# Attention over a cached K and V: probabilities transposed in 32x32 blocks by VectorE, the first 16 units' values by pairs, and a quarter of wo projected earlier

**Chip and metric.** One core of one Trainium2 chip. The time is that of the device for one launch, in microseconds (us). Executions carry a state, fast or slow (a slow one lies over 1.5% above the fastest of its kernel); only fast ones are compared, and each ratio is to the kernel before as it ran in the same job. PE is TensorE, DVE is VectorE, ACT is ScalarE, SP issues the loads.

## The reference, cut

```python
B, Sq, D = 8, 4, 512
Hq, Hkv, Sk, Dh = 32, 8, 2048, 128
q = (x @ wq).reshape(B, Sq, Hq, Dh).transpose(0, 2, 1, 3)
k, v = (jnp.repeat(t, Hq // Hkv, axis=1) for t in (k_cache, v_cache))
p = softmax(einsum("bhqd,bhkd->bhqk", q, k) * Dh ** -0.5)
o = einsum("bhqk,bhkd->bhqd", p, v)
return o.transpose(0, 2, 1, 3).reshape(B, Sq, Hq * Dh) @ wo      # all bfloat16
```

K and V are 33.5 MB each, wq and wo 4.2 MB each: 75.5 MB are read for little arithmetic.

## The kernel before

The work is cut into 32 units: one pair of K/V heads of one batch, 1 MB of K and 1 MB of V. For each unit PE transposes K (as f32 words, two bf16 in one), DVE copies the result out of PSUM (`kt`), PE makes scores, ACT takes the exponential and its row sums, PE transposes the probabilities back so that keys lie on the partitions, ACT copies those to `probs`, and PE multiplies with V. `norms` turns the row sums into reciprocals, once for two units.

```python
def transpose_part(u, t):                 # four parts to a unit
    for j in range(JT):
        nc.tensor.transpose(kp[:, j, :], k4[:, w : w + 128], ident4[:, :])
    nc.vector.tensor_copy(out=k_t..., in_=kp...)               # 128x1024 bf16
...
def probs_to_keys(u):
    for j in range(JT):
        nc.tensor.transpose(pt[:, j, :], s_sbs[u][:, j, :, :]..., ident[:, :])
    for g in range(2):
        nc.scalar.copy(out=pr[rows, :, g, :], in_=pt[rows, :, :]...)
...
def values(u):                            # 32 matmuls of 32 columns
    for i in range(C):
        nc.tensor.matmul(o_ps[:, :], lhsT=vs[u][:, 2 * (t * JT + j) + c, :], rhs=pr[:, i, :, :]..., ...)
...
for n in range(NU + A):                   # A = 2: values run two units behind the K transposes
    w = n - A
    transpose_part(n, 0..1); scores(n - 1); transpose_part(n, 2..3)
    if w >= 0:
        values(w)
        if w % 2 == 0: norms(w)
        finish(w)
    probs_to_keys(n - 1)
    load_ready(...)                       # lets SP issue what may be issued
```

A `manual_schedule` keeps the order of the source.

The softmax here doesn't subtract the row's maximum and nothing guards it: scores larger than these inputs give would overflow.

## Time and profile before

| | before |
|---|---|
| time, median of three runs | 190.3 us (189.22 to 192.44) |
| span of the profiled run | 187.5 us |
| PE, DVE, ACT busy | 78%, 59%, 37% |
| bytes of the load queue | 75.55 MB, 96.3% of the span of 16 DMA engines |

### The profile page before, as it was taken

Reading aid. Unit: us, or ns where it says so; the run is one execution under the profiler, and the core shown is the slowest. Engines: PE = TensorE matmul, PEld = TensorE weight load, DVE = VectorE, ACT = ScalarE, POOL = GpSimd, SP = SyncE. Lnnn points to the kernel's source line nnn. Section 1 sums busy time; section 2 is a strip of 40 time slices with the busy share of each in tenths; the row PEclk is TensorE's granted clock in tenths of the full one; section 3 lists DMA queues with packets and bytes.
Section 4 is the critical chain, followed back from the end, with each engine's and each line's share of the span. In section 5 each row is a group of like instructions: output and inputs, shape, how many; then the busy total and the mean of one; then the engine's idle time right before and its main releaser. Section 6 shows DMA issues by size and latency. Waiting matters only on the chain.

```text
span 187.5 us, 5467 instructions
## 1 busy us (share of the span) xinstructions
PE 146.1 (78%) x2386; PEld 118.4 (63%) x2386; DVE 110.0 (59%) x225; ACT 69.1 (37%) x200; POOL 4.6 (2%) x9
## 2 busy tenths in 40 slices
PE   0524789999999788898788888788799888887382
PEld 0511248888797667786676766666587677666271
DVE  0850376878877566587565657575277766674020
ACT  2001146446464443153444443423344443435200
POOL 8100000000000000000000000000000000000000
PEclk9999999999999999999999999999699999999879
DMA  5998999999999999999999999999999999999970
GB/s 203 468 447 376 426 425 426 426 419 425 426 423 425 419 428 425 426 423 426 428 419 426 425 426 421 432 421 423 423 426 421 428 425 421 426 425 404 400 292 14
DMA packets 10983, 75.90 MB, mean 405 GB/s; under 512 B 1288, under 2 KB 1448, under 8 KB 2600
## 3 DMA queue, kind: packets, MB, share of 16 engines
q1 hardware_dynamic: 10912, 75.55, 96.3%
q8 instruction: 18, 0.29, 0.6%
q14 instruction: 5, 0.04, 0.1%
q10 hardware_dynamic: 48, 0.02, 0.0%
HBM read 75.53 MB, written 0.03 MB: 403 GB/s over the span
## 4 chain that ended last, share of the span: by engine, by line
DMA 81%; PE 13%; DVE 2%; issue 1%; ACT 1%; SPq 0%
DMA k_sb<-in_k_cache_dram 50%; DMA v_sb<-in_v_cache_dram 10%; DMA wo_m<-in_wo_dram 9%; DMA x_sb<-in_x_dram 7%; PE kp L199 6%; DMA wo_sb<-in_wo_dram 4%; PE psq L220 2%; PE s_ps L269 2%; DVE kt L201 1%; PE qtp L230 1%; ACT q_nat L227 1%; PE pse L244 1%; PE pt L288 0%; PE l_ps L311 0%; PE o_ps L329 0%
## 5 line engine op out<-in xcount | busy, mean ns | idle before, releaser
L201 DVE COPY kt<-kp 128x1024 bf16<-128x1024 bf16 x128 | 82.6, 685 | 35.2 <-PE kp L199 35.1
L199 PE MATMUL kp<-ident,k_sb 128*128 128x128 f32 x512 | 73.2, 289 | 20.0 <-DMA k_sb<-in_k_cache_dram 18.4
L199 PEld LDWEIGHTS kp<-ident,k_sb 128*128 128x128 f32 x512 | 58.6, 147 | 31.7 <-issue 15.9
L294 ACT COPY probs<-pt 64x512 bf16<-64x512 bf16 x64 | 37.1, 579 | 52.7 <-PE pt L288 52.3
L280 ACT ACTIVATE s_sb<-s_ps 128x256 bf16<-128x256 f32 x64 | 23.9, 379 | 30.6 <-PE s_ps L269 19.9
L329 PE MATMUL o_ps<-probs,v_sb 128*128 128x32 bf16 x1024 | 30.7, 177 | 1.7 <-DMA v_sb<-in_v_cache_dram 1.7
L329 PEld LDWEIGHTS <-v_sb 128*128 128x128 bf16 x1024 | 29.9, 96 | 3.0 <-DMA v_sb<-in_v_cache_dram 2.2
L269 PE MATMUL s_ps<-kt,q_bd 128*32 128x256 bf16 x512 | 21.3, 286 | 0.0
L269 PEld LDWEIGHTS <-q_bd 128*32 128x32 bf16 x512 | 10.8, 96 | 6.4 <-issue 5.5
L319 DVE RECIPROCAL r_sb<-l_ps 128x64 f32<-128x64 f32 x16 | 8.9, 557 | 8.6 <-PE l_ps L311 8.6
L280 ACT ACTIVATION_READ_ACCUMULATOR s_sb<-s_ps 128x1 f32 x64 | 12.7, 198 | 0.0
L288 PE MATMUL pt<-ident,s_sb 128*128 128x128 bf16 x128 | 12.3, 218 | 0.0
L311 PE MATMUL l_ps<-by_gq,ones 128*128 128x64 f32 x32 | 6.9, 297 | 5.3 <-DVE by_gq L304 5.3
L340 DVE TENSOR_TENSOR oT<-o_ps,r_sb 128x32 bf16<-128x32 f32 x32 | 6.1, 191 | 6.3 <-PE o_ps L329 5.7
L311 PEld LDWEIGHTS l_ps<-by_gq,ones 128*128 128x128 f32 x32 | 4.8, 188 | 6.8 <-DVE by_gq L304 5.0
L288 PEld LDWEIGHTS <-s_sb 128*128 128x128 bf16 x128 | 8.9, 104 | 0.0
L227 ACT ACTIVATE q_nat<-psq 128x512 bf16<-128x512 f32 x2 | 1.2, 597 | 18.7 <-PE psq L220 18.7
L304 DVE TENSOR_TENSOR by_gq<-l_sb,by_q 128x64 f32<-128x64 f32 x16 | 3.4, 216 | 2.1 <-ACT s_sb L280 2.1
L236 DVE COPY qT_all<-qtp 128x128 bf16<-128x128 bf16 x8 | 1.2, 216 | 5.8 <-PE qtp L230 5.8
L220 PE MATMUL psq<-wq_sb,xT_sb 128*32 128x512 bf16 x32 | 3.8, 628 | 0.3 <-DVE xT_sb L214 0.3
L461 ACT CAST out_sb<-out_ps 64x256 bf16<-64x256 f32 x1 | 0.4, 365 | 9.8 <-PE out_ps L405 9.8
L211 PE MATMUL xtp<-ident,x_sb 32*128 32x32 bf16 x4 | 0.3, 191 | 4.4 <-DMA x_sb<-in_x_dram 4.4
(48 smaller groups left out, 45.2 us busy)
## 6 DMA issues: line engine op xcount, KB each, us to landing
k_sb<-in_k_cache_dram SPq DMA_DIRECT2D x32, 1024.0 KB, 19.6
v_sb<-in_v_cache_dram SPq DMA_DIRECT2D x32, 1024.0 KB, 12.7
wq_sb<-in_wq_dram SPq DMA_DIRECT2D x1, 4096.0 KB
wo_sb<-in_wo_dram SPq DMA_DIRECT2D x4, 512.0 KB
wo_sb<-in_wo_dram SPq DMA_DIRECT2D x4, 256.0 KB, 8.2
wo_m<-in_wo_dram SPq DMA_DIRECT2D x1, 640.0 KB
wo_e<-in_wo_dram SPq DMA_DIRECT2D x8, 40.0 KB
wo_n<-in_wo_dram SPq DMA_DIRECT2D x1, 64.0 KB, 18.4
```

What stands on the lines that cost most here:

```text
L199: nc.tensor.transpose(kp[:, j, :], k4[:, w : w + 128], ident4[:, :])
L201: nc.vector.tensor_copy(out=k_t[:, :, :, :].rearrange("k j s e -> k (j s e)"), in_=kp[:, :, :].rearrange("k j s -> k (j s)").bitcast(BF16),)
L220: nc.tensor.matmul(psq[k * T : (k + 1) * T, :], lhsT=xT_sb[:, r, :], rhs=wq_sb[:, r, n : n + rep * Dh], start=(r == 0), stop=(r == R - 1),)
L269: nc.tensor.matmul(s_ps[t * 32 : (t + 1) * 32, :, g, :], lhsT=q_bd[:, p, e, b, g, :, :], rhs=kt[(u, t)][:, :, g * 64 : (g + 1) * 64, e], s ...
L280: nc.scalar.activation(out=s_sb[:, :, g, :], in_=s_ps[:, :, g, :], func=EXP, accum_out=l_sbs[u][:, u % 2, g : g + 1])
L288: nc.tensor.transpose(pt[:, j, :], s_sbs[u][:, j, :, :].rearrange("q g s -> q (g s)"), ident[:, :])
L294: nc.scalar.copy(out=pr[rows, :, g, :], in_=pt[rows, :, :].rearrange("s j (c q) -> s (j c) q", q=HQ),)
L304: nc.vector.tensor_tensor(out=by_gq[:, :, :, :], in0=l_sbs[u][:, :, :].unsqueeze(3).to_broadcast([128, 2, 2, HQ]), in1=by_q[:, :].unsqueez ...
L311: nc.tensor.matmul(l_ps[:, :, :].rearrange("d u q -> d (u q)"), lhsT=ones[:, :], rhs=by_gq[:, :, :, :].rearrange("k u g q -> k (u g q)"), ...
L319: nc.vector.reciprocal(r_sb[:, :, :], l_ps[:, :, :])
L329: nc.tensor.matmul(o_ps[:, :], lhsT=vs[u][:, 2 * (t * JT + j) + c, :], rhs=pr[:, i, :, :].rearrange("s g q -> s (g q)"), start=(i == 0), s ...
L340: nc.vector.tensor_tensor(out=oT[(p + 1) // 2][:, :, (p == 2) * 1, b, :], in0=o_pss[u][:, :].rearrange("d (h s) -> d h s", h=HP), in1=r_sb ...
```

## The change

It takes work from PE and ACT, and is meant to shorten what follows the last loads. Not shown in the cut: the scores are laid out for transposes within 32x32 blocks, one exponential of 512 columns replaces two of 256, the PSUM space of the old transposes goes to a fourth buffer for `kp`, and the loads of the first quarter of wo are put into the list of the other loads, at the place in which they already stood. Its core:

```diff
-    for j in range(JT):
-        nc.tensor.transpose(pt[:, j, :], ...)
     for g in range(2):
-        nc.scalar.copy(out=pr[rows, :, g, :], in_=pt[rows, :, :]...)
+        nc.vector.transpose(out=pr[rows, :, g, :], in_=s_sbs[u][rows, :, :]...)   # 32x32 blocks
...
-    nc.vector.tensor_copy(out=k_t..., in_=kp...)
+    (nc.scalar.copy if part == 3 else nc.vector.tensor_copy)(out=kt[(u, t)]..., in_=kp...)
...
+def values2(u):                            # units u and u + 1 together, first 16 units
+    for i in range(2):
+        nc.vector.tensor_tensor(out=by_row[:, i, :, :, :], in0=l_sbs[u]..., in1=by_q..., op=mult)
+    nc.tensor.matmul(l_ps[:, :], lhsT=by_row..., rhs=ones[:, 0:1], ...)
+    nc.vector.reciprocal(r_sb[:, :], l_ps[:, :])
+    for c in range(0, C, 2):
+        for i in range(2):                 # 256 columns each
+            nc.tensor.matmul(o_ps[i * 64 : (i + 1) * 64, :], lhsT=probs[(u + i) % 3][:, c : c + 2, :, :]...,
+                             rhs=vs[u + i][:, c : c + 2, :]..., ...)
+    nc.scalar.mul(out=o_sb..., in_=o_ps[:, :], mul=r_sb[:, 0:1])
+def finish2(u): ...                        # two f32 matmuls fold the halves into oT
...
     transpose_part(n, 2..3)
+    probs_to_keys(n - 1)                   # was the last thing of the step
     if w >= 0:
-        values(w) ...
+        if w >= NU - NS: values(w) ...     # NS = 16
+        elif w % 2 == 1: values2(w - 1)
-    probs_to_keys(n - 1)
-    load_ready(min(n + 1, NU), max(w + 1, 0))
+    load_ready(min(n + 1, NU), max(w + 1 if w >= NU - NS else (w + 1) // 2 * 2, 0))
...
     if w == NU - 2:
         project(0, WE, WM + 1)
+        project(1, 0, 8)
-to_tokens(2); project(1, 0, 4); to_wo_rows(2); project(1, 4, 4)
+to_tokens(2); to_wo_rows(2)
```

More of the change, by code (lines that the diff above doesn't have):

```diff
@@ L38 @@
     J = C // 2
-    JT = J // 4
+    JT = J // 2
+    NS = 16
     HP = 2 * rep
@@ L60 @@
     vpool = ctx.enter_context(tc.tile_pool(name="vpool", bufs=VB))
-    ktpool = ctx.enter_context(tc.tile_pool(name="ktpool", bufs=6))
+    ktpool = ctx.enter_context(tc.tile_pool(name="ktpool", bufs=3))
     small = ctx.enter_context(tc.tile_pool(name="small", bufs=2))
-    psum_k = ctx.enter_context(tc.tile_pool(name="psum_k", bufs=3, space=bass.MemoryType.PSUM))
+    psum_k = ctx.enter_context(tc.tile_pool(name="psum_k", bufs=4, space=bass.MemoryType.PSUM))
     psum_s = ctx.enter_context(tc.tile_pool(name="psum_s", bufs=1, space=bass.MemoryType.PSUM))
-    psum_t = ctx.enter_context(tc.tile_pool(name="psum_t", bufs=1, space=bass.MemoryType.PSUM))
     psum_o = ctx.enter_context(tc.tile_pool(name="psum_o", bufs=1, space=bass.MemoryType.PSUM))
@@ L99 @@
     ident = const.tile([128, 128], BF16, name="ident")
-    by_q = const.tile([128, HQ], FP32, name="by_q")
+    by_q = const.tile([128, 2, HQ], FP32, name="by_q")
+    fold = const.tile([128, 2, 2, NQ], FP32, name="fold")
     ones = const.tile([128, 128], FP32, name="ones")
-    pad = const.tile([128, 96], BF16, name="pad")
+    pad = const.tile([128, 64], BF16, name="pad")
     probs = [const.tile([128, C, 2, HQ], BF16, name=f"probs{i}") for i in range(3)]
@@ L155 @@
         if u == NU + 2:
-            loads.append(("m", 0))
+            loads += [("m", 0), ("w", 0), ("w", 4)]
         if u >= KA - 1 and u - KA + 1 < NU:
@@ L164, in load_ready @@
             kind, u = loads[-1]
-            if kind in "em":
+            if kind in "emw":
                 loads.pop()
-                load_wo_e(u) if kind == "e" else load_wo_m()
+                load_wo_e(u) if kind == "e" else load_wo_m() if kind == "m" else load_wo(1, u, 4)
                 continue
@@ L188, with transpose_part @@
     nc.vector.tensor_reduce(
-        out=by_q[:, :], in_=ident4[:, :].rearrange("p (c q) -> p q c", q=HQ), axis=AX, op=ADD
-    )
-    kt = {}
-    def transpose_part(u, t):
-        kp = psum_k.tile([128, JT, 128], FP32, tag="k", name="kp")
+        out=by_q[:, :, :],
+        in_=ident4[:, :].rearrange("p (g c q) -> p g q c", g=2, q=HQ),
+        axis=AX,
+        op=ADD,
+    )
+    nc.vector.memset(fold[:, :, :, :], 0.0)
+    for c in range(2):
+        nc.vector.tensor_copy(
+            out=fold[:, c, :, :],
+            in_=ident4[:, :].rearrange("p (u c q) -> p c u q", u=2, c=2)[:, c, :, :],
+        )
+    kt = {}
+    def transpose_part(u, part):
+        t, half = divmod(part, 2)
+        if half == 0:
+            kt[(u, t)] = ktpool.tile([128, JT, 128, 2], BF16, tag="kt", name="kt")
+        kp = psum_k.tile([128, JT // 2, 128], FP32, tag="k", name="kp")
         k4 = ks[u][:, :, :].rearrange("s c d -> s (c d)").bitcast(FP32)
-        for j in range(JT):
-            w = (t * JT + j) * 128
+        for j in range(JT // 2):
+            w = (part * JT // 2 + j) * 128
             nc.tensor.transpose(kp[:, j, :], k4[:, w : w + 128], ident4[:, :])
-        k_t = ktpool.tile([128, JT, 128, 2], BF16, tag="kt", name="kt")
-        nc.vector.tensor_copy(
-            out=k_t[:, :, :, :].rearrange("k j s e -> k (j s e)"),
+        (nc.scalar.copy if part == 3 else nc.vector.tensor_copy)(
+            out=kt[(u, t)][:, half * JT // 2 : (half + 1) * JT // 2, :, :].rearrange(
+                "k j s e -> k (j s e)"
+            ),
             in_=kp[:, :, :].rearrange("k j s -> k (j s)").bitcast(BF16),
         )
-        kt[(u, t)] = k_t
-    for t in range(4):
-        transpose_part(0, t)
+    for part in range(4):
+        transpose_part(0, part)
     xtp = psum_o.tile([128, R, T], BF16, tag="o", name="xtp")
@@ L227 @@
         nc.scalar.mul(out=q_nat[:, half, :], in_=psq[:, :], mul=scale)
-        qtp = psum_t.tile([128, rep, 4, B, Sq], BF16, tag="t", name="qtp")
+        qtp = psum_l.tile([128, rep, 4, B, Sq], BF16, tag="l", name="qtp")
         for h in range(rep):
@@ L241 @@
         for e in range(2):
-            pse = (psum_t.tile([128, 2, B, 2, HQ], FP32, tag="t", name="pse")
+            pse = (psum_l.tile([128, 2, B, 2, HQ], FP32, tag="l", name="pse")
                    if e else psum_s.tile([128, 2, B, 2, HQ], FP32, tag="s", name="pse"))
@@ L264, in scores @@
         p, b = units[u]
-        s_ps = psum_s.tile([128, JT, 2, 64], FP32, tag="s", name="s_ps")
-        for g in range(2):
+        s_ps = psum_s.tile([128, J, 32], FP32, tag="s", name="s_ps")
+        for t in range(2):
             for e in range(2):
-                for t in range(4):
+                for y in range(4):
                     nc.tensor.matmul(
-                        s_ps[t * 32 : (t + 1) * 32, :, g, :],
-                        lhsT=q_bd[:, p, e, b, g, :, :],
-                        rhs=kt[(u, t)][:, :, g * 64 : (g + 1) * 64, e],
+                        s_ps[y * 32 : (y + 1) * 32, t * JT : (t + 1) * JT, :],
+                        lhsT=q_bd[:, p, e, b, y // 2, :, :],
+                        rhs=kt[(u, t)][:, :, y * 32 : (y + 1) * 32, e],
                         start=(e == 0),
@@ L275, in scores @@
                     )
-        s_sb = small.tile([128, JT, 2, 64], BF16, tag="s_sb", name="s_sb")
+        s_sb = small.tile([128, J, 32], BF16, tag="s_sb", name="s_sb")
         if u % 2 == 0:
-            l_sbs[u] = l_sbs[u + 1] = small.tile([128, 2, 2], FP32, tag="l_sb", name="l_sb")
-        for g in range(2):
-            nc.scalar.activation(
-                out=s_sb[:, :, g, :], in_=s_ps[:, :, g, :], func=EXP, accum_out=l_sbs[u][:, u % 2, g : g + 1]
-            )
+            l_sbs[u] = l_sbs[u + 1] = small.tile([128, 2], FP32, tag="l_sb", name="l_sb", bufs=3)
+        nc.scalar.activation(
+            out=s_sb[:, :, :], in_=s_ps[:, :, :], func=EXP,
+            accum_out=l_sbs[u][:, u % 2 : u % 2 + 1],
+        )
         s_sbs[u] = s_sb
     def probs_to_keys(u):
-        pt = psum_t.tile([128, JT, 128], BF16, tag="t", name="pt")
-        for j in range(JT):
-            nc.tensor.transpose(
-                pt[:, j, :], s_sbs[u][:, j, :, :].rearrange("q g s -> q (g s)"), ident[:, :]
-            )
         pr = probs[u % len(probs)]
@@ L293, in probs_to_keys @@
             rows = slice(g * 64, (g + 1) * 64)
-            nc.scalar.copy(
-                out=pr[rows, :, g, :],
-                in_=pt[rows, :, :].rearrange("s j (c q) -> s (j c) q", q=HQ),
+            nc.vector.transpose(
+                out=pr[rows, :, g, :], in_=s_sbs[u][rows, :, :].rearrange("q j s -> q (j s)")
             )
     r_sbs = {}
+    o_pss = {}
     def norms(u):
@@ L305, in norms @@
             out=by_gq[:, :, :, :],
-            in0=l_sbs[u][:, :, :].unsqueeze(3).to_broadcast([128, 2, 2, HQ]),
-            in1=by_q[:, :].unsqueeze(1).unsqueeze(1).to_broadcast([128, 2, 2, HQ]),
+            in0=l_sbs[u][:, :].unsqueeze(2).unsqueeze(2).to_broadcast([128, 2, 2, HQ]),
+            in1=by_q[:, :, :].unsqueeze(1).to_broadcast([128, 2, 2, HQ]),
             op=mybir.AluOpType.mult,
@@ L320, in norms @@
         r_sbs[u] = r_sbs[u + 1] = r_sb
-    o_pss = {}
     def values(u):
@@ L326, in values @@
         o_ps = psum_o.tile([128, NQ], FP32, tag="o", name="o_ps")
-        for i in range(C):
-            j, t, c = i // 8, i // 2 % 4, i % 2
+        for c in range(C):
             nc.tensor.matmul(
                 o_ps[:, :],
-                lhsT=vs[u][:, 2 * (t * JT + j) + c, :],
-                rhs=pr[:, i, :, :].rearrange("s g q -> s (g q)"),
-                start=(i == 0),
-                stop=(i == C - 1),
+                lhsT=vs[u][:, c, :],
+                rhs=pr[:, c, :, :].rearrange("s g q -> s (g q)"),
+                start=(c == 0),
+                stop=(c == C - 1),
             )
@@ L344, in finish, with finish2 @@
             op=mybir.AluOpType.mult,
+        )
+    o_sbs = {}
+    def values2(u):
+        by_row = small.tile([128, 2, 2, 2, HQ], FP32, tag="by_row", name="by_row")
+        for i in range(2):
+            nc.vector.tensor_tensor(
+                out=by_row[:, i, :, :, :],
+                in0=l_sbs[u][:, i : i + 1].unsqueeze(2).unsqueeze(2).to_broadcast([128, 2, 2, HQ]),
+                in1=by_q[:, :, :].unsqueeze(1).to_broadcast([128, 2, 2, HQ]),
+                op=mybir.AluOpType.mult,
+            )
+        l_ps = psum_l.tile([128, 1], FP32, tag="l", name="l_ps")
+        nc.tensor.matmul(
+            l_ps[:, :],
+            lhsT=by_row[:, :, :, :, :].rearrange("k u c g q -> k (u c g q)"),
+            rhs=ones[:, 0:1],
+            start=True,
+            stop=True,
+        )
+        r_sb = small.tile([128, 1], FP32, tag="r1_sb", name="r1_sb")
+        nc.vector.reciprocal(r_sb[:, :], l_ps[:, :])
+        o_ps = psum_o.tile([128, 2 * Dh], FP32, tag="o", name="o_ps")
+        for c in range(0, C, 2):
+            for i in range(2):
+                nc.tensor.matmul(
+                    o_ps[i * 64 : (i + 1) * 64, :],
+                    lhsT=probs[(u + i) % len(probs)][:, c : c + 2, :, :].rearrange(
+                        "s c g q -> s (c g q)"
+                    ),
+                    rhs=vs[u + i][:, c : c + 2, :].rearrange("s c d -> s (c d)"),
+                    start=(c == 0),
+                    stop=(c == C - 2),
+                )
+        o_sb = small.tile([128, 2, Dh], FP32, tag="o_sb", name="o_sb", bufs=1)
+        nc.scalar.mul(
+            out=o_sb[:, :, :].rearrange("q c d -> q (c d)"), in_=o_ps[:, :], mul=r_sb[:, 0:1]
+        )
+        o_sbs[u] = o_sb
+    def finish2(u):
+        p, b = units[u]
+        f_ps = psum_l.tile([128, 2, NQ], FP32, tag="l", name="f_ps")
+        for c in range(2):
+            nc.tensor.matmul(
+                f_ps[:, :, :].rearrange("d u q -> d (u q)"),
+                lhsT=o_sbs[u][:, c, :],
+                rhs=fold[:, c, :, :].rearrange("k u q -> k (u q)"),
+                start=(c == 0),
+                stop=(c == 1),
+            )
+        nc.vector.tensor_copy(
+            out=oT[(p + 1) // 2][:, :, (p == 2) * 1, b : b + 2, :],
+            in_=f_ps[:, :, :].rearrange("d u (h s) -> d h u s", h=HP),
         )
@@ L414 @@
         w = n - A
-        for t in range(2):
+        for part in range(2):
             if 0 < n < NU:
-                transpose_part(n, t)
+                transpose_part(n, part)
+        if 2 <= w <= NU - NS and w % 2 == 0:
+            finish2(w - 2)
         if 0 <= n - 1 < NU:
             scores(n - 1)
-        for t in range(2, 4):
+        for part in range(2, 4):
             if 0 < n < NU:
-                transpose_part(n, t)
+                transpose_part(n, part)
+        if 0 <= n - 1 < NU:
+            probs_to_keys(n - 1)
         if w >= 0:
@@ L426 @@
                 to_tokens(p // 2)
-            values(w)
+            if w >= NU - NS:
+                values(w)
+                if w % 2 == 0:
+                    norms(w)
+                finish(w)
+            elif w % 2 == 1:
+                values2(w - 1)
             if p in (1, 3) and b == 2:
                 to_wo_rows(p // 2)
-            if w % 2 == 0:
-                norms(w)
-            finish(w)
-        if 0 <= n - 1 < NU:
-            probs_to_keys(n - 1)
-        load_ready(min(n + 1, NU), max(w + 1, 0))
+        load_ready(min(n + 1, NU), max(w + 1 if w >= NU - NS else (w + 1) // 2 * 2, 0))
         if w == NU - 1 - VB:
             assert not loads
-            load_wo(1, 0, 4)
-            load_wo(1, 4, 4)
             load_wo(2, 0, 4)
@@ L450 @@
             project(0, WE, WM + 1)
+            project(1, 0, 8)
     to_tokens(2)
-    project(1, 0, 4)
     to_wo_rows(2)
-    project(1, 4, 4)
     project(2, 0, 4)
```

## The prediction

> **What bounds the kernel now.** I read the page's shares and its forty slices first, then the chain that ended last, the waits of the DMA queue, the groups of instructions, and the timeline of the last 12 us.
>
> ```profile
> span 187.5 us, 5467 instructions
> PE 146.1 (78%) x2386; PEld 118.4 (63%) x2386; DVE 110.0 (59%) x225; ACT 69.1 (37%) x200; POOL 4.6 (2%) x9
> DMA  5998999999999999999999999999999999999970
> GB/s 203 468 447 376 426 425 426 426 419 425 426 423 425 419 428 425 426 423 426 428 419 426 425 426 421 432 421 423 423 426 421 428 425 421 426 425 404 400 292 14
> q1 hardware_dynamic: 10912, 75.55, 96.3%
> DMA 81%; PE 13%; DVE 2%; issue 1%; ACT 1%; SPq 0%
> ```
>
> No engine is full, but the transfers are: from the second slice to the 38th the rate lies near 425 GB/s and the DMA row reads 8 or 9. The chain that ended last is 81% DMA. 75.55 MB at 425 GB/s are 177.8 us; the other 9.7 us of the span are the first slice (203 instead of 425 GB/s, 2.4 us lost), small dips, and the end (after the last landing at 183.86 us by the chain, 3.6 us for the last matmuls, one copy and the output).
>
> The queue's own waits say how safe that stream is:
>
> ```profile
> SPq L124 <- DMA v_sb<-in_v_cache_dram: 47.2, 22, 3.1
> SPq L114 <- DMA k_sb<-in_k_cache_dram: 44.0, 22, 2.1
> SPq L124 <- PE kp L199: 5.9, 19, 0.4
> ```
>
> The issuer nearly always waits for an earlier transfer to land (91 us in these two lines), and hardly ever for a buffer that an engine has to give back (5.9 us, never more than 0.4 at once). A K load lands 19.6 us after its issue, that is 8 loads of 1 MB at 2.46 us. So some 19 us of work lie queued in front of the memory, and an engine that returns a buffer one or two us later is not seen in the rate.
>
> The groups that the change touches:
>
> ```profile
> L201 DVE COPY kt<-kp 128x1024 bf16<-128x1024 bf16 x128 | 82.6, 685 | 35.2 <-PE kp L199 35.1
> L294 ACT COPY probs<-pt 64x512 bf16<-64x512 bf16 x64 | 37.1, 579 | 52.7 <-PE pt L288 52.3
> L280 ACT ACTIVATE s_sb<-s_ps 128x256 bf16<-128x256 f32 x64 | 23.9, 379 | 30.6 <-PE s_ps L269 19.9
> L319 DVE RECIPROCAL r_sb<-l_ps 128x64 f32<-128x64 f32 x16 | 8.9, 557 | 8.6 <-PE l_ps L311 8.6
> L227 ACT ACTIVATE q_nat<-psq 128x512 bf16<-128x512 f32 x2 | 1.2, 597 | 18.7 <-PE psq L220 18.7
> ```
>
> And the end, from the timeline:
>
> ```profile
> 176.43 1.11 PE L405 MATMUL out_ps<-wo_m,oM 128*32 128x256 bf16 x10 [3.10 <-DMA wo_m<-in_wo_dram]
> 177.80 1.04 PE L329 MATMUL o_ps<-probs,v_sb 128*128 128x32 bf16 x32
> 180.19 0.68 DVE L359 COPY nat_sb<-nat 32x1024 bf16<-32x1024 bf16 x1 [1.13 <-PE nat L353]
> 180.93 0.67 PE L375 MATMUL perm<-ident,nat_sb 32*128 32x32 bf16 x8 [0.34 <-DVE nat_sb L359]
> 181.53 2.15 PE L405 MATMUL out_ps<-wo_sb,oP 128*32 128x256 bf16 x36
> 183.91 0.40 PE L405 MATMUL out_ps<-wo_sb,oP 128*32 128x256 bf16 x4 [0.23 <-DMA wo_sb<-in_wo_dram]
> 184.34 0.36 ACT L461 CAST out_sb<-out_ps 64x256 bf16<-64x256 f32 x1 [9.80 <-PE out_ps L405]
> ```
>
> The last unit's values start at 177.80, its tokens are copied, permuted, and then 36 projection matmuls run at 0.06 us each. PE comes to the last four with 0.23 us to spare before their weights land. That small slack is the only place where I expect the change to be felt.
>
> [...] No transpose by VectorE is in the trace before. [...] The trace has 379 ns for 256 and 597 ns for 512 elements, 0.85 ns an element[...].
>
> **The change, part by part.** One unit (a pair of heads of one batch) brings 2 x 1.05 MB, at 425 GB/s 4.93 us. That is the budget that each engine has per unit.
>
> *VectorE.* It loses a quarter of the kt copies: 4 x 0.685 = 2.74 us become 3 x 0.685 = 2.06 us per unit. It gains two transposes of 64x512. [...] The rest in units 16 to 31 stays: half of (557 + 216), plus 191, 0.58 us. Sum 4.06 us against 3.32 before. In units 0 to 15 the reciprocal shrinks from 64 elements to one, the per-unit product goes, two small products and one 64-element copy per pair come: some 0.35 us (estimated from the 0.2 us that such small instructions take), sum 3.83. Over 32 units 126 us, plus the 10 or so of setup and tokens: busy 130 to 137 us, about 72%. Within 4.93, so beside the transfers.
>
> *ScalarE.* Loses 2 x 579 = 1.16 us of copies per unit; two exponentials of 379 (and two reads of the accumulator at 198) become one of about 597 and one read; gains one 1024-element copy, 597 + 512 x 0.85 = 1.03 us. From 2.3 us per unit to 1.8; far from the budget.
>
> *TensorE.* Loses four transposes per unit (12.3 us over all, about 0.22 us of path each unit). Values by pairs: 16 matmuls of 256 columns with 64 weight columns per unit in place of 32 of 32 columns. A score matmul also has 256 columns, four side by side, 16 in about 0.6 us; with two side by side 16 should take about 1.0 to 1.2 us, against 0.95 now. The fold adds two f32 matmuls per pair (one such of 64 columns takes 0.43 us at L311). So the first half is even and the second some 0.2 us a unit lighter; the stretch from 60 to 150 us had PE busy 75.6 of 90 us. Also beside the transfers.
>
> *Buffers.* V tiles of the first 16 units come free in pairs, so every second one a unit later. I followed both lists of loads by hand: the order of the loads is identical, element for element. At a V load's natural issue the values that read its buffer were done about 1.5 units (7 us) earlier; a unit later and a step longer leaves about 2 us, and behind that stand the 19 us of queued transfers. v(6) is the tightest: issued at 39.5 us now, its pair is done around 39 to 40 us. No gap in the stream.
>
> *The wo quarter.* Since the order of loads is the same (the trace has the last V issued at 154.2, the 64 rows at 156.6, wo_m at 159.1, the quarters from 161.6), nothing lands earlier. What moves is PE's program: 16 projection matmuls of the first quarter of wo_sb now stand ahead of the last unit's values. wo_m lands at 176.38, the last of wo_sb at 183.86, so its 3.15 MB come at 420 GB/s and the first quarter's second half lands near 176.4 + 2.5 = 178.9 us. PE, which now starts the last values at 177.80, will start them near 178.9 + 8 x 0.06 to 0.11, that is 179.4 to 179.8. From there as now: values to oP ready took 181.92 - 177.80 = 4.1 us, and values to the end of the permutation 3.8. The 16 matmuls that lay in this chain are gone from it (0 to 0.3 us saved). So the 32 left start at about 183.1 to 183.5 and need 1.9 us: end 185.0 to 185.4 in place of 184.31. All weights have landed by 183.86. PE, not the last transfer, ends the kernel: **+0.7 to +1.1 us**, less the saving, so about +0.7.
>
> **Sum.** Middle 0, head 0, end +0.7: span 188.2. The times of before are 190.3 in the median with 189.2 and 192.4 beside it, and the profiled run's 189.3; the fast level is probably 189.3 to 190.3. I say **190.5 us**, about +0.3%.
>
> **Rivals.**
> 1. *VectorE becomes the bound.* The budget breaks when 2.06 + 0.58 + 2T passes 4.93, at T = 1.14 us a transpose, 60% over my estimate. For it: no such instruction is in the trace, and the output is strided (16 elements on, 16 off). Against: the 64x512 strided copies on ScalarE were no slower than dense ones (579 against 597 ns). At T = 1.5 the middle would run at 5.6 us a unit and the time would be past 205 us. I give 4%.
> 2. *V buffers by pairs starve the stream.* It needs delays of more than the queued 19 us. For it: the catch-up from 25 to 60 us, where PE was busy 33.6 of 35 us. Against: never over 0.4 us waiting on an engine. Would cost 0.5 to 3 us; 5%.
> 3. *The new order at the end is hidden or wins.* If the end of the stream were PE-bound, doing 16 matmuls early would save up to 16 x 0.06 = 1 us. Against: PE waited 0.23 us for the last weights, so at most 0.2 us can be won there, to 189.8. 25%.
> 4. *Less work makes it faster by over 2%.* That needs 186.5 us, under 177.8 + 2.4 + 3.6 + the 1.8 us between the span and the time plus dips. Hardly possible: 3%, for noise.
>
> **Range and chances.** The spread of before alone is 189.2 to 192.4; with the end's 0 to +1.1 I take 188.8 to 192.2. Faster by over 2% 0.03, within 2% 0.92, slower by over 2% 0.05.
>
> **What would show it right or wrong.** The rate row again near 425 from slice 5 to 36 and a queue that waits for landings: the middle is right. 64 transposes of about 0.7 us on VectorE, its share about 70%, ScalarE near 33%: costs right. At the end a PE wait for wo_sb before the last values, these starting near 179.5, and no wait for wo_sb at the last projection: the last step right. If the last landing comes well before or after 183.9 us, or the queue waits over 2 us at a time on the values of a pair, my account of the stream is wrong; if the last values start before 178.5, my account of the end is.

## The result

| | before | changed |
|---|---|---|
| time, median of four runs | 191.37 us (189.22 to 194.15) | 209.94 us (207.57 to 210.29) |
| span of the profiled run | 187.5 us | 208.1 us |

The ratio of the changed kernel to the one before is 1.104 (95% interval 1.089 to 1.119): 10% slower. A ratio here is the mean time of one kernel's fast runs over that of the other's fast runs of the same rounds, so not quite the ratio of the medians. My range ended at 192.2.

### The profile page after: what moved, and what is told of

It reads as the page before. It is cut to its first block, busy times and chain, and to the rows that moved or that the text cites. A ratio compares the mean times of both kernels' runs of the same rounds, so it can differ in the third digit from the quotient of the medians.

```text
span 208.1 us, 4749 instructions
## 1 busy us (share of the span) xinstructions
PE 155.3 (75%) x2034; PEld 124.3 (60%) x2034; DVE 131.4 (63%) x260; ACT 63.4 (30%) x112; POOL 4.6 (2%) x9
## 4 chain that ended last, share of the span: by engine, by line
PE 56%; DVE 28%; DMA 7%; ACT 4%; issue 3%; SPq 0%; ACTq 0%
PE kp L215 24%; DVE probs L306 15%; PE o_ps L383 11%; DVE kt L216 9%; PE s_ps L286 7%; DMA x_sb<-in_x_dram 7%; PE out_ps L472 4%; ACT kt L216 3%; PE psq L236 2%; PE l_ps L371 2%; PE l_ps L323 2%; PE f_ps L402 2%; DVE by_row L364 1%; PE o_ps L338 1%; DVE by_gq L316 1%
## 5 line engine op out<-in xcount | busy, mean ns | idle before, releaser
L216 DVE COPY kt<-kp 128x1024 bf16<-128x1024 bf16 x96 | 62.5, 686 | 38.3 <-PE kp L215 37.6
L306 DVE STREAM_TRANSPOSE probs<-s_sb 64x512 bf16<-64x512 bf16 x64 | 45.0, 703 | 1.2 <-ACT s_sb L296 0.5
L216 ACT COPY kt<-kp 128x1024 bf16<-128x1024 bf16 x32 | 32.4, 1012 | 15.6 <-PE kp L215 15.6
L296 ACT ACTIVATE s_sb<-s_ps 128x512 bf16<-128x512 f32 x32 | 19.1, 598 | 57.8 <-PE s_ps L286 57.8
L383 PE MATMUL o_ps<-v_sb,probs 128*64 128x256 bf16 x256 | 23.0, 356 | 0.0
L371 PE MATMUL l_ps<-ones,by_row 128*128 128x1 f32 x16 | 3.6, 295 | 23.3 <-DVE by_row L364 23.3
L383 PEld LDWEIGHTS <-probs 128*64 128x64 bf16 x256 | 18.1, 144 | 1.9
L338 PEld LDWEIGHTS <-v_sb 128*128 128x128 bf16 x512 | 15.0, 96 | 1.2 <-issue 1.0
L338 PE MATMUL o_ps<-probs,v_sb 128*128 128x32 bf16 x512 | 15.3, 176 | 0.4 <-DVE oT L349 0.4
L323 PEld LDWEIGHTS l_ps<-by_gq,ones 128*128 128x128 f32 x16 | 2.4, 188 | 10.4 <-DVE by_gq L316 9.1
L296 ACT ACTIVATION_READ_ACCUMULATOR s_sb<-s_ps 128x1 f32 x32 | 6.2, 194 | 0.0
L472 PE MATMUL out_ps<-wo_sb,oP 128*32 128x256 bf16 x48 | 5.3, 404 | 0.0
## 6 DMA issues: line engine op xcount, KB each, us to landing
v_sb<-in_v_cache_dram SPq DMA_DIRECT2D x32, 1024.0 KB, 12.7
```

Of the source, the lines that this page charges most:

```text
L216: (nc.scalar.copy if part == 3 else nc.vector.tensor_copy)(out=kt[(u, t)][:, half * JT // 2 : (half + 1) * JT // 2, :, :].rearrange("k j s ...
L296: nc.scalar.activation(out=s_sb[:, :, :], in_=s_ps[:, :, :], func=EXP, accum_out=l_sbs[u][:, u % 2 : u % 2 + 1],)
L306: nc.vector.transpose(out=pr[rows, :, g, :], in_=s_sbs[u][rows, :, :].rearrange("q j s -> q (j s)"))
L323: nc.tensor.matmul(l_ps[:, :, :].rearrange("d u q -> d (u q)"), lhsT=ones[:, :], rhs=by_gq[:, :, :, :].rearrange("k u g q -> k (u g q)"), ...
L338: nc.tensor.matmul(o_ps[:, :], lhsT=vs[u][:, c, :], rhs=pr[:, c, :, :].rearrange("s g q -> s (g q)"), start=(c == 0), stop=(c == C - 1),)
L371: nc.tensor.matmul(l_ps[:, :], lhsT=by_row[:, :, :, :, :].rearrange("k u c g q -> k (u c g q)"), rhs=ones[:, 0:1], start=True, stop=True,)
```

## The profile after

The page of the changed kernel, to hold against the page lines in the prediction:

```profile
span 208.1 us, 4749 instructions
PE 155.3 (75%) x2034; PEld 124.3 (60%) x2034; DVE 131.4 (63%) x260; ACT 63.4 (30%) x112; POOL 4.6 (2%) x9
PEclk9999999699795875999879996999999999699787
GB/s 302 403 384 428 428 428 424 428 427 422 428 422 428 411 428 238 427 285 339 427 168 424 351 424 320 417 422 420 427 424 422 428 425 425 421 405 342 0 3 6
PE 56%; DVE 28%; DMA 7%; ACT 4%; issue 3%; SPq 0%; ACTq 0%
```

No engine is full here either; DVE's 131 us are what I forecast. But the chain that ended last, 81% DMA before, is now PE and DVE in turn, and from the 16th slice (78 us) the rate has holes. PEclk has ten slices under 8; the page of before has two. The groups:

```profile
L306 DVE STREAM_TRANSPOSE probs<-s_sb 64x512 bf16<-64x512 bf16 x64 | 45.0, 703 | 1.2 <-ACT s_sb L296 0.5
L216 ACT COPY kt<-kp 128x1024 bf16<-128x1024 bf16 x32 | 32.4, 1012 | 15.6 <-PE kp L215 15.6
L371 PE MATMUL l_ps<-ones,by_row 128*128 128x1 f32 x16 | 3.6, 295 | 23.3 <-DVE by_row L364 23.3
```

The new instructions cost about what the prediction counts: 703 ns a transpose, for which it has about 0.7 us, a time that no trace had shown by then and on which its sums for VectorE rest; and 1012 ns ACT's copy, against 1030 worked out from the trace before. With the measured times a unit of the second half sums to 3 x 0.686 + 2 x 0.703 + 0.58 = 4.04 us on DVE, where it has 4.06. The third row is the strange one: a sum that takes 3.6 us in all had PE idle for 23.3 us before it, waiting for `by_row`, a product of 128x64 elements. The queue's waits:

```profile
SPq L128 <- PE o_ps L383: 71.9, 8, 11.8
SPq L128 <- PE o_ps L338: 34.2, 10, 5.2
```

The issuer of loads, which before waited for landings, now waits 106 us for the values of a unit to give back a V buffer. Is that cause or echo? The timeline of one pair shows the order of events (start, duration, engine, line, operation, count, in brackets the idle time before and what ended it):

```profile
72.21 1.09 PE L215 MATMUL kp<-ident,k_sb 128*128 128x128 f32 x8
72.43 1.89 DVE L216 COPY kt<-kp 128x1024 bf16<-128x1024 bf16 x3
74.34 1.42 DVE L306 STREAM_TRANSPOSE probs<-s_sb 64x512 bf16<-64x512 bf16 x2
75.78 0.36 DVE L364 TENSOR_TENSOR by_row<-l_sb,by_q 128x64 f32<-128x64 f32 x2
76.20 0.58 PE L371 MATMUL l_ps<-ones,by_row 128*128 128x1 f32 x2 [2.90 <-DVE by_row L364]
76.71 3.63 PE L383 MATMUL o_ps<-v_sb,probs 128*64 128x256 bf16 x32
80.27 1.97 PE L215 MATMUL kp<-ident,k_sb 128*128 128x128 f32 x8
```

PE is done with the step's K transposes at 73.3 us. Its next instruction is the sum by ones, ahead of the values. That needs `by_row`, which DVE comes to only after three kt copies and two transposes that belong to other units: 75.8 us. PE stands for 2.90 us, though the probabilities that the values need were transposed by 72.4 us, and the row sums that `by_row` needs were read out by 70.5. Then everything on PE takes nearly twice its time: 3.63 us for 32 matmuls that take 1.94 in other pairs of the same trace, and 1.97 for K transposes that took 1.09 before the wait. While PE does this, DVE has next to nothing to do (one reciprocal, then 4.4 us idle before its next copy). The two engines take turns instead of working side by side. The same stretch by the view of windows (length, busy time of PE, weight loads, DVE, ACT and POOL, granted clock, DMA share, GB/s):

```profile
66.80:80.30 13.50, 10.60 (x103) 8.79 (x103) 7.35 (x14) 3.88 (x7) 0.00 (x0) 0.75 0.95 396
```

The clock granted in this stretch was 0.75 (1 is full speed). From the starts of `by_row` (37.7 to 124.9 us) the mean pair took 12.5 us; the transfers need 2 x 4.93 = 9.86. The last pair's result is scaled at 128.2 us; in the run by_row_early below, whose PE waits more than 0.2 us in only one pair, at 102.6. So the changed kernel is 25.6 us late when the paired half ends. From there to the start of the last values it takes 70.2 us, the other, bound by the transfers, 76.5; so 6 us are won back and 19 stay. At the end:

```profile
195.07 1.25 PE L472 MATMUL out_ps<-wo_m,oM 128*32 128x256 bf16 x10
198.40 0.98 PE L338 MATMUL o_ps<-probs,v_sb 128*128 128x32 bf16 x32
201.65 3.38 PE L472 MATMUL out_ps<-wo_sb,oP 128*32 128x256 bf16 x32
```

No weights are waited for here; PE is simply late, and its last 32 projections run at 0.106 us each where those before the change took 0.06.

**Theories.** (1) The place of a small product in DVE's order makes PE stand, and the idle time lowers PE's clock: wait and clock make the loss. (2) The paired matmuls are too long in themselves. (3) V buffers given back in pairs starve the stream. (4) DVE's transposes make the path too long, wherever they stand. (5) The new order at the end has a part.

## The experiments

Twelve kernels ran. All outputs are right. "Changed" is the kernel after the change.

### One part alone, three times

**all_single**: changed with `NS = 32`, so no pairs.

```diff
-    NS = 16
+    NS = 32
```

> The changed kernel with no unit in pairs (transposes by VectorE and the new order at the end stay). Theory 1, that in the paired units PE stands some 2.9 us a pair for a small VectorE product queued behind copies and transposes and then runs at a lower clock: the middle is again bound by the transfers, DMA near 425 GB/s throughout, ratio to before 0.99 to 1.02, span 187 to 190. Theory 4, that the transposes on VectorE alone make the path too long: still 4% or more slower than before. The second half of the changed kernel ran at 4.1 us a unit, under the 4.93 of the transfers, which speaks for theory 1.

Measured: ratio 1.015 (1.007 to 1.023), span 191.1; DMA near 425 GB/s throughout (426 from 140 to 170 us), and the issuer waits 91 us for K and V to land, as before the change. All but 1.5 of the 10.4% go with the pairs, while the transposes stay on DVE: against (4). Its span lies about 1 us above the 187 to 190 that I expected; see order_alone for its end.

**pairs_alone**: the kernel before, plus `values2`, `finish2` and the paired release of V, with PE's transposes.

```diff
-            values(w)
+            if w >= NU - NS: values(w)
+            elif w % 2 == 1: values2(w - 1)
```

> The kernel before with the first 16 units' values by pairs and chunks, V buffers given back in pairs, probabilities still transposed by PE and copied by ScalarE, old order at the end. Theory 1: VectorE has four kt copies in a step but no transposes before the small product, so PE waits about 1.5 us a pair instead of 2.9, the clock mostly stays up, and a pair takes about 9.5 to 10.5 us against the transfers' 9.86: ratio 1.00 to 1.04. Theory 2, that the paired matmuls themselves are too long, or theory 3, that V buffers given back in pairs starve the stream: ratio 1.07 or more, as in the changed kernel.

Measured: ratio 1.001 (0.992 to 1.010), span 186.7. The pairs' starts are 9.95 us apart. The wait for the product:

```profile
PE l_ps L371 <- DVE by_row L364: 10.1, 8, 1.6
```

1.26 us a pair, and all eight groups of paired values took 1.94 us. Against (2): the paired matmuls are fine. Neither pairs alone nor transposes alone cost much; the loss belongs to the two together. The two transposes put 1.42 us more into the queue in front of `by_row`, and PE's wait is 2.9 us instead of 1.3.

**order_alone**: the kernel before with the first quarter of wo_sb projected ahead of the last values.

```diff
             project(0, WE, WM + 1)
+            project(1, 0, 8)
-    to_tokens(2); project(1, 0, 4); to_wo_rows(2); project(1, 4, 4)
+    to_tokens(2); to_wo_rows(2)
```

> The kernel before with only the new order at the end (the first quarter of wo_sb projected ahead of the last unit's values). My predicted cost of 0.7 us: last values start near 179.5 instead of 177.8, last projection ends near 185.1 instead of 184.3, span 188.0 to 188.6. Rival, that PE makes the place up: span within 0.2 us of 187.5. Either is within the noise of the times, so the trace decides.

Measured: span 188.4 in the profiled run; ratio 1.012 (1.001 to 1.022) from two fast runs of its own (190.3 and 192.7 us), too wide to size it. The trace does:

```profile
177.93 1.98 PE L405 MATMUL out_ps<-wo_sb,oP 128*32 128x256 bf16 x16
179.84 1.04 PE L329 MATMUL o_ps<-probs,v_sb 128*128 128x32 bf16 x32
183.41 1.92 PE L405 MATMUL out_ps<-wo_sb,oP 128*32 128x256 bf16 x32
```

The last values start 2.04 us later than before and the projections end at 185.3 instead of 184.3. My forecast had PE wait for wo_sb here; it did not. The 16 projections that were moved ran in one piece behind those of wo_m and wo_n, but slowly (1.98 us, where the last 32 took 1.92), after a wait of 2.68 us for wo_m. In all_single the last group is worse off:

```profile
183.24 3.60 PE L472 MATMUL out_ps<-wo_sb,oP 128*32 128x256 bf16 x32
```

There the 32 projections took 3.60 us in place of 1.92, another 1.7 us. That slowness does not belong to the new order: transposes_alone below, with the old one, has its last 40 projections in 4.21 us, and norm_last, with the new one, its 32 in 1.92. So by this trace (5) is true in kind, worth 1 us in a kernel that the transfers bound.

**transposes_alone**: changed with `NS = 32` and the old order at the end.

> The changed kernel with no unit in pairs and the old order at the end: only the transposes by VectorE, with one kt copy in four on ScalarE. Middle bound by the transfers as in the run with the new order at the end; last values near 177 to 178 instead of 179.5, and the end 1 to 3 us earlier than in that run (span 191.1), at 187 to 189; ratio to before 0.99 to 1.01.

Measured: span 188.1, last values at 177.1 us, ratio 0.996 (0.988 to 1.004). Two of its four runs were slow, so the ratio rests on two. As expected: the first part of the change by itself costs nothing that these runs resolve.

### The place of the product

**by_row_early**: changed; the product of a pair goes to DVE at the top of its step.

```diff
         w = n - A
+        if 0 <= w < NU - NS and w % 2 == 1:
+            rows2(w - 1)          # the two tensor_tensor that make by_row, moved out of values2
         for part in range(2):
```

> The changed kernel with the small product of a pair issued to VectorE at the top of its step, ahead of that step's copies and transposes; nothing else differs. Theory 1: PE's 23 us of waiting for it go, the paired values take about 1.9 us each instead of 3.3, pairs take under 9.9 us, and the ratio to before falls from 1.10 to 0.99 to 1.02. Theories 2, 3 and 4: the ratio stays above 1.06.

Measured: ratio 1.005 (1.000 to 1.010), span 188.9. The same instructions on the same engines, two of 0.2 us each moved ahead of some 3.3 us of others, and 10% come back. One pair of it:

```profile
59.88 0.22 DVE L362 TENSOR_TENSOR by_row<-l_sb,by_q 128x64 f32<-128x64 f32 x1
60.01 1.88 DVE L216 COPY kt<-kp 128x1024 bf16<-128x1024 bf16 x3
60.34 0.28 PE L376 MATMUL l_ps<-ones,by_row 128*128 128x1 f32 x2
60.55 1.94 PE L388 MATMUL o_ps<-v_sb,probs 128*64 128x256 bf16 x32
61.81 1.42 DVE L306 STREAM_TRANSPOSE probs<-s_sb 64x512 bf16<-64x512 bf16 x2
```

The sum follows without a wait, and the values (60.55 to 62.5) overlap with DVE's copies and transposes. Pairs are 9.2 us apart in the mean, so now they wait for the transfers:

```profile
GB/s 203 463 444 390 423 428 428 420 432 418 427 423 427 427 423 428 420 430 423 427 430 418 432 416 425 428 416 435 420 432 423 423 427 421 434 417 404 398 150 7
```

**norm_last**: changed; product and sum after the values, on both engines. DVE's order in the step stays as in the changed kernel.

```diff
-    by_row ...; l_ps ...; r_sb ...
     o_ps: the 32 matmuls
+    by_row ...; l_ps ...; r_sb ...
     o_sb ...
```

> The changed kernel with the small product and the sum by ones of a pair issued after the pair's values in place of before them, on VectorE and on PE; VectorE's order of copies, transposes and product within the step is the same as in the changed kernel. Theory 1 (PE stands for the product and the clock drops): PE goes straight from the K transposes to the values, which take about 1.9 us each, and then waits under 1 us; ratio to before 0.99 to 1.03. If the product's place in VectorE's row were not the matter but VectorE's load, the ratio would stay above 1.06.

Measured: ratio 0.994 (0.987 to 1.000), span 187.7. PE still waits for the product, 1.0 us a pair, but after the values instead of before:

```profile
62.38 1.94 PE L365 MATMUL o_ps<-v_sb,probs 128*64 128x256 bf16 x32
65.34 0.38 PE L383 MATMUL l_ps<-ones,by_row 128*128 128x1 f32 x2 [1.02 <-DVE by_row L376]
```

All paired values took 1.94 us. With DVE's work and order unchanged, (4) falls for good: what counted was which of PE's instructions stood behind the wait.

### Wait or clock

**warm**: changed, with ten matmuls of 256 columns put in front of the sum. They fill part of PE's wait; their result is overwritten.

```diff
+        for _ in range(10):
+            nc.tensor.matmul(o_ps[:, :], lhsT=ident[:, :], rhs=vs[u][:, 0:2, :]..., start=True, stop=True)
         nc.tensor.matmul(l_ps[:, :], lhsT=by_row..., rhs=ones[:, 0:1], ...)
```

> The changed kernel with ten extra matmuls of 256 columns, whose result is overwritten, in the time in which PE waits for the product; the wait's end is not moved. If the lower clock after the wait is a good part of the loss: the paired values take 1.9 us in place of 3.3 on average, the K transposes after them 1.0 in place of up to 1.9, a pair takes about 10.5 us in place of 12.3, ratio to before 1.01 to 1.05. If the wait alone is the loss and the clock is a side effect: the ratio stays 1.09 to 1.11.

Measured: ratio 1.068 (1.061 to 1.075). This missed both expectations. 1.8 us of each wait stayed idle in the mean, and PE still ran slowly in every second pair: values of 1.94 us and of 2.46 or more in turn. Hence:

**warm22**: the same with 22.

> As the run with ten extra matmuls, with 22, so that PE is busy through nearly the whole wait of 2.9 us [...]; the product arrives when it did. With ten the clock still fell at times (values 1.87 or 2.4 us) and a pair took 11.9 us in place of 12.5. If the lower clock is the larger part: all paired values take 1.9 us, the K transposes after them 1.0, a pair takes 10.5 to 10.9 us, ratio to before 1.01 to 1.04. If the wait alone is the larger part: a pair stays above 11.5 us, ratio 1.06 or more.

Measured: ratio 1.042 (1.035 to 1.048), a pair every 10.9 us, and all eight groups of values at 1.94:

```profile
57.11 2.57 PE L372 MATMUL o_ps<-v_sb,ident 128*128 128x256 bf16 x22
60.17 0.38 PE L378 MATMUL l_ps<-ones,by_row 128*128 128x1 f32 x2 [0.49 <-DVE by_row L364]
60.49 1.94 PE L389 MATMUL o_ps<-v_sb,probs 128*64 128x256 bf16 x32
62.35 1.09 PE L215 MATMUL kp<-ident,k_sb 128*128 128x128 f32 x8
```

More work made the kernel 12 us faster. The product still arrives 2.9 us after the K transposes, so the wait as such is all there; only the clock is kept up (0.97 granted from 25 to 120 us, where the changed kernel had 0.88 from 25 to 128). Of the 10.4% lost, about 6.2 were the clock and 4.2 the wait. These are from two jobs; in warm22's own job after_old_end, the changed kernel but for its end, lost 10.0, which would make it 5.8 and 4.2. In two of the eight pairs the 22 matmuls outlast the wait, so 4.2 is rather too high. In pairs: 12.5 to 10.9 us is the clock, 10.9 to 9.86 the wait.

### The rivals

**more_v**: changed with seven V buffers, which gives back the one unit by which pairs return them later.

```diff
-    VB = 6
+    VB = 7
```

> The changed kernel with seven V buffers in place of six, which gives back the one unit by which the paired release comes later. Theory 3 (V buffers given back in pairs starve the stream): the ratio falls to 1.05 or lower. Theory 1: the compute path is the bound and the queue's wait only its echo, so the ratio stays 1.08 to 1.11, and the first low slice of the rate comes later, by about a unit.

Measured: ratio 1.110 (1.100 to 1.119). The first deep hole in the rate moved from the 16th slice to the 19th, 16 us later (I had said about one unit, 5 us):

```profile
GB/s 299 399 398 424 427 429 421 426 429 421 427 423 427 429 426 409 420 399 287 427 172 427 374 402 356 377 420 423 426 427 426 426 421 422 385 360 42 0 3 6
```

The time did not fall: (3) is refuted. SP's wait for V buffers went from 106 us to 65, and 32 us of waiting for K buffers came instead. So the wait for V buffers was an echo of a slow PE.

**after_old_end**: changed with only the order at the end undone (as in order_alone, reversed).

> The changed kernel with only the order at the end undone. The compute path ends the kernel, all of wo has landed long before, so 16 matmuls ahead of the last values or behind them cost the same: span within 1 us of 208.1, ratio 1.09 to 1.11. If the new order had a part in the 20 us, it would fall below 1.08.

Measured: ratio 1.100 (1.091 to 1.108), span 207.6. Where PE ends the kernel anyway, the order is worth nothing that the runs resolve: against (5) as a part of the 10%.

### Is there a version that beats both?

**early_old_end** and **norm_last_old_end**: by_row_early and norm_last with the old order at the end.

> The changed kernel with the product issued at the top of the step and the old order at the end: span 186.5 to 187.8, against 188.9 with the new order; ratio 0.985 to 1.005.

> The best version so far (product and sum after the values) with the old order at the end. Middle bound by the transfers, the last values near 177, no cold stretch of projections after them: span 186.5 to 187.5, about 1 us less than with the new order (187.7); ratio to before 0.985 to 1.0. If it is under 0.99 with its interval it beats before[...].

Measured: 0.995 (0.988 to 1.002) and 0.999 (0.992 to 1.006). Their fastest runs are 188.6 and 188.5 us beside 188.8 for the kernel before. Neither beats the kernel before by anything that these runs resolve, which is what a stream of 75.5 MB at 425 GB/s allows. Nor do the times show the 1 us of the order at the end: undoing it goes with a lower ratio in two versions (all_single 1.015 to 0.996, by_row_early 1.005 to 0.995) and a higher one in the third (norm_last 0.994 to 0.999), each from two jobs. That 1 us rests on order_alone's trace.

| kernel | pair, us | PE's wait for the product, us a pair | paired values, us | ratio |
|---|---|---|---|---|
| changed | 12.5 | 2.9 | 1.94 to 3.63, mean 2.9 | 1.104 |
| warm | 11.9 | 1.8 idle, 1.3 filled | 1.94 to 3.36, mean 2.3 | 1.068 |
| warm22 | 10.9 | 0.5 idle, 2.6 filled | 1.94 | 1.042 |
| pairs_alone | 9.95 | 1.26 | 1.94 | 1.001 |
| norm_last | 9.2 | 1.0, after the values | 1.94 | 0.994 |
| by_row_early | 9.2 | none, but for one pair (2.1) | 1.94, that pair 3.52 | 1.005 |

## Why the prediction was wrong

- **What bounds the kernel before**: right. Every version whose PE does not stand ahead of the values runs at the transfers' rate (by_row_early 425 to 426 GB/s from 25 to 170 us).
- **Costs of single instructions**: right. Transposes 703 ns (said about 0.7 us, not shown by a trace then), ACT's copy 1012 (1030), DVE busy 131 us (130 to 137). The paired values take 0.97 us a unit in pairs_alone, whose mean granted clock was 0.99 (said 1.0 to 1.2). One small reading does not come out: the four transposes taken from PE are given as 0.22 us a unit, but 12.3 us over 32 units are 0.38.
- **The end**: the numbers right, the path in part by luck. I said that the last values would start at 179.4 to 179.8 and PE's last projection end at 185.0 to 185.4; order_alone has 179.84 and 185.3. But I had PE wait for wo_sb before the values, and it did not: the 16 projections took 1.98 us, about twice the time of an equal number later, and so lasted as long as I thought the landing would. In the changed kernel itself the end never was as forecast: the loads were over by 192.5 us, and PE came to its last values at 198.40.
- **The step that failed** is "TensorE ... So the first half is even ... Also beside the transfers", and with it "No gap in the stream". I set each engine's busy time per unit against 4.93 us, and every one fitted. That is a test of load. It says nothing of the order in which PE and DVE wait for each other. The diff showed that order: `values2` begins with a product on DVE and a sum of it on PE, and `probs_to_keys` had moved ahead of it. Walking one step in the order of the program with durations that I had or had estimated (3 x 0.64 + 1.42 + 0.4 us on DVE before the sum, of which PE's own K transposes cover some 0.9) would have shown a stand of nearly 3 us in every pair. What the runs showed in its place: PE stood 2.9 us a pair behind DVE's queue, a pair took 12.5 us instead of at most 9.86, and without that stand (by_row_early, norm_last) the loss was gone.
- **The second omission** is that a wait on PE costs more than itself. In the changed kernel the values behind a wait of 2.90 us took 3.63 us where they otherwise take 1.94, in a stretch with a granted clock of 0.75 (66.8 to 80.3 us); slow values came after gaps of 2.27 to 3.57 us there. By warm22 this made about 6 of the 10 points.
- **Rivals**: I gave 4% to a bound on DVE and 5% to starved V buffers. Neither happened, though the second is what the queue's waits look like. (I also gave the V loads the 19 us that a K load takes to land; a V load landed after 12.7.) I had no rival in which two engines take turns.

## What to carry to other kernels

A budget of busy time per engine is necessary and not sufficient: for each instruction that an engine must pass in order, ask which other engine's queue its input stands in, and behind what. Put small products that another engine waits for at the head of the queue, or put the wait behind work that needs nothing from it. When a wait on PE appears, count the lower clock after it as well (here about 6 of the 10 points), and take a load queue that waits for buffers as an echo until an extra buffer has been tried (here a seventh V buffer, and the ratio stayed at 1.110).

## What the traces leave open

- When the values behind a gap are slow. In the changed kernel the gaps of PE before the sum were 2.27 to 3.57 us, and length alone did not decide: after 2.27, 2.90, 2.90 and 3.57 us the paired values took 3.3 to 3.6 us, after 2.90 and 3.36 us in other pairs 1.94 us, as in pairs_alone. In warm two gaps of 1.81 us in successive pairs were followed by 2.46 us and by 1.94 us. Gaps of up to 1.6 us (all eight of pairs_alone) never went with slow values. No run here settles what makes equal gaps end differently.
- The profiled run of norm_last_old_end, counted as slow, took 198.1 us where the same kernel otherwise took 188.5 to 190.6. In its chain the K load issued at 57.7 us took 22.2 us to land, the three after it 19.5 to 20.6. It is left out of the ratios, as is that of early_old_end (191.7 us); the cause stays open.
